# Identity transposes in TensorE's waits of batch 0's attention, and at_l's products behind the others, in a packed attention with a softplus FFN

## The chip, the cores and the metric

The kernel runs on one core of a Trainium2 chip. The metric is the device time of one execution in microseconds (us). Three runs of the kernel before took 799.06, 800.18 and 801.27 us; their median is 800.18 us. All inputs lie in HBM and the output goes back there.

## The reference

q, k and v have the shape 8 x 8 x 576 x 64 (batch, heads, sequence, head size), p has 8 x 8 x 32 x 64. Per batch and head a softmax attention packs k and v into 32 rows for p's queries, and a second attention reads these packed rows with q. The result of all heads goes through an FFN with a softplus in between.

```
p_packed = sm_attn(p, k, v)                # 32 rows for each head
out = sm_attn(q, p_packed, p_packed)       # 576 rows for each head
x = out.transpose(0, 2, 1, 3).reshape(B * S, H * D)    # 4608 x 512
h = x @ w_in                               # w_in 512 x 2048
g = np.maximum(h, 0.0) + np.log1p(np.exp(-np.abs(h)))
return (g @ w_out).astype(np.float32)      # w_out 2048 x 512
```

`sm_attn` scales the scores by 1/8, subtracts the row's maximum, and divides by the sum plus 1e-9. w_in and w_out come in 64-bit floats.

## The kernel before, in words

**Staging.** Batch 0's attention runs first and alone; then the FFN runs batch by batch, in units: a unit is one of the 16 blocks of 128 FFN columns of one batch. RUNS gives their order: blocks 0 to 7 of batch 0, all blocks of batch 1, blocks 8 to 15 of batch 0, then the batches 2 to 7. Between the products of a unit the kernel steps through the attention of the next batch (`attention`, a generator) and, in the first units, through the conversion of the weights (`convert`, a generator too).

**attention(b)** works on two groups of four heads (g = 0, 1). `transposed` makes T_k and T_q: three TensorE transposes into a PSUM bank and a copy on ScalarE. `scores1` multiplies T_k with pT; ScalarE copies the scores (tile a1, printed as a), VectorE takes the maximum, ScalarE the exponential. `a1_transposed` turns the weights on TensorE into the bank psa, and ScalarE copies them to a1T. `packed` multiplies them with v (bank psp). For the second attention `scores2` multiplies T_q with the packed rows (pt), VectorE transposes the scores (L324), `softmax2_exp` and `softmax2_div` normalise them with VectorE and ScalarE, and a last VectorE transpose makes aT (L348). c = 0, 1 are the two halves of the 576 rows.

**convert** makes 32-bit weights out of the 64-bit ones, for each x_i (of w_in) and x_o (of w_out): a DMA load, m and r on ScalarE (L182, L186), t on VectorE (L188, L193), a sum on GpSimd (L201), and for x_o the two parts wo_h (ScalarE, L222) and wo_l (VectorE, L228).

**weights(b)** splits aT into two parts of reduced precision: at_h is a cast on ScalarE (L469), at_l the difference on VectorE (L470), for c = 0 with g = 0, 1, then for c = 1. **make_m** multiplies the packed rows with w_in (bank psm) and splits the product into mh (ScalarE) and ml (VectorE), for two blocks at once in the first units. **gemm1(b, f, res)** then adds, for each half c and in one PSUM accumulation, six products over g: mh with at_h, mh with at_l, ml with at_h. `softplus` reads the result, and two units later `gemm2_tile` multiplies gh and gl with wo_h and wo_l into the bank acc.

**Order.** TensorE's instructions stand as the program writes them. The other engines' queues are ordered by a scheduler when the program is built; each engine then works through its queue in that order. DMA loads are issued on the sync queue. During batch 0's attention `bank` hands out six PSUM banks in turn (four of ps_acc, two of ps_m), afterwards the two of ps_m.

Of the kernel before, what the change touches and what calls it, by code (L numbers as in the profile page):

```python
# [9 lines left out]
F32 = mybir.dt.float32  # L10
# [16 lines left out]
def pack_attention_then_softplus_ffn(  # L27
# [10 lines left out]
    nc = tc.nc  # L38
# [3 lines left out]
    P = 128  # L42
# [3 lines left out]
    C = S // 2  # L46
    G = H * J // P
# [24 lines left out]
    ident = const.tile([P, P], F32, name="ident")  # L72
# [17 lines left out]
    def bank(nm):  # L90
        if spare:
            spare.append(spare.pop(0))
            pool, tag = spare[-1]
            return pool.tile([P, 512], F32, tag=tag, name=nm)
        return ps_m.tile([P, 512], F32, tag="m", name=nm)
# [11 lines left out]
    def pack_transposed(bg, t):  # L107
        for o in range(0, H, HG):
            ps = bank(f"ppt_{bg}_{o}")
            for i in range(HG):  # L110
                nc.tensor.transpose(ps[:D, i * P:(i + 1) * P], t[:, o + i, :], ident)
            dst = pT[:, o:o + HG, :].rearrange("x h j -> x (h j)")
            nc.vector.tensor_copy(dst[:D], ps[:D])
            nc.scalar.copy(dst[D:], ps[:D])
# [41 lines left out]
    def convert(order):  # L156
# [56 lines left out]
        for n in range(len(order) + 1):  # L213
# [13 lines left out]
            if w == "o":  # L227
# [3 lines left out]
                made.add((w, i))  # L231
                yield


    def transposed(nm, b, g, hh):

        src = loaded[nm, b, g]
        ps = bank(f"psT_{nm}_{b}_{g}_{hh}")
        for i in range(HS):
            nc.tensor.transpose(  # L240
                ps[:, i * NP:(i + 1) * NP],
                src[:, hh, 2 * i:2 * i + 2, :].rearrange("x s d -> x (s d)"),
                ident[:NP, :NP],
            )
        dst = work.tile([P, C], F32, tag="T", name=f"T_{nm}_{b}_{g}_{hh}", bufs=4)
        nc.scalar.copy(dst, ps[:, :C])  # L246
        return dst
# [105 lines left out]
    def attention(b):  # L353
# [34 lines left out]
        pp[0] = packed(b, 0, a1T, rs0)  # L388
        load("k", b + 1, 0)
        yield  # L390
        qT.append(transposed("q", b, 0, 0))
        yield
        a1T = work.tile([NP, SI, P], F32, tag="a1T", name=f"a1T_{b}_1", bufs=1)
# [66 lines left out]
    def weights(b):  # L460

        at_h = work.tile([P, G, S], F32R, tag="at_h", name=f"at_h_{b}", bufs=1)
        at_l = work.tile([P, G, S], F32R, tag="at_l", name=f"at_l_{b}", bufs=1)
        res[b]["at"] = (at_h, at_l)
        for c in range(2):
            cols = slice(c * C, (c + 1) * C)
            for g in range(G):
                aT = res[b]["aT"][g, c]
                nc.scalar.copy(at_h[:, g, cols], aT)  # L469
                nc.vector.tensor_tensor(  # L470
                    at_l[:, g, cols], aT, at_h[:, g, cols].bitcast(F32), op=ALU.subtract
                )
# [39 lines left out]
    def gemm1(b, f, res):  # L512

        at_h, at_l = res["at"]
        phs = []
        for c in range(2):
            ph = ps_h.tile([P, 512], F32, tag="h", name=f"ph_{b}_{f}_{c}")
            phs.append(ph[:, :C])
            i = 0
            for g in range(G):  # L520
                mh, ml, o = res["m"][f][g]
                ms = slice(o, o + P)
                cs = slice(c * C, (c + 1) * C)
                for x, y in ((mh, at_h), (mh, at_l), (ml, at_h)):
                    nc.tensor.matmul(  # L525
                        ph[:, :C], x[:, ms], y[:, g, cs],
                        start=(i == 0), stop=(i == 3 * G - 1),
                    )
                    i += 1
        return phs  # L530

    def halves(nm):
# [111 lines left out]
    res = [{"pt": [], "aT": {}, "m": {}} for _ in range(B)]  # L644

    spare += [(ps_acc, "acc")] * NT + [(ps_m, "m")] * 2
    pack_transposed(0, pt)
    due = 0.0
    for st, _ in enumerate(attention(0)):
# [3 lines left out]
            due -= 1  # L653
    make_m(0, 0, m_cols(0), res[0])
    weights(0)

    spare.clear()
    cdue = 0.0
    gs, acc = {}, None
# [94 lines left out]
```

## Time and profile before

| | |
|---|---|
| median of three runs | 800.18 us (799.06 to 801.27) |
| the profiled execution, its own time | 801.79 us |
| its span, first to last instruction | 800.0 us |
| TensorE busy | 761.3 us, 95% |
| VectorE busy | 514.6 us, 64% |
| ScalarE busy | 468.4 us, 59% |
| GpSimd busy | 92.6 us, 12% |
| mean granted TensorE clock over the span | 0.985 |

Busy times are sums over the whole span. The kernel has stages with different limits, so the table alone does not tell what limits a stage; the rows further down are cut by time. The granted clock is a share of 2.4 GHz. Ends of matmuls are modelled, so a row's length on TensorE is that of its last instruction plus the starts before it.

### The profile page before, as it was taken

To read this page: it belongs to the slowest core of one execution; us is meant where nothing else is said; L and a number is where in the kernel's file an instruction comes from. 1 tells how busy PE (TensorE), PEld (TensorE's weight loads), DVE (VectorE), ACT (ScalarE), POOL (GpSimd) and SP (SyncE) were. 2 spreads that over 40 slices of the span, in tenths; PEclk is the share of its full clock that TensorE was granted. 3 is DMA by queue.
4 is the path that set the end of the run, shared out by engine and by line. 5 is a ranking of instruction groups with operands and counts; after the bars stand their busy time and mean duration, and the time that the engine had idled before them with its cause. 6 is when DMAs were issued, how large, how long until landed. Compare 5 with 4: busy or idle time off the path is not lost.

```text
span 800.0 us, 14909 instructions
## 1 busy us (share of the span) xinstructions
PE 761.3 (95%) x5664; PEld 602.2 (75%) x5664; DVE 514.6 (64%) x1180; ACT 468.4 (59%) x1189; POOL 92.6 (12%) x166
## 2 busy tenths in 40 slices
PE   6369998999999999999999999999999999999997
PEld 4246676777788787877788777878778777878886
DVE  2685898855687547764677456764587546764544
ACT  5668787866563565575555465566556355555540
POOL 1412234400000000000000000000000000000010
PEclk9967999999999999999999999999999999999999
DMA  9985655501513112122212122132211210010002
GB/s 230 236 218 161 167 164 162 141 9 55 169 32 83 43 30 61 30 83 60 61 30 64 33 60 60 31 84 60 60 30 28 70 31 1 1 53 1 1 2 66
DMA packets 40519, 59.28 MB, mean 74 GB/s; under 512 B 5120, under 2 KB 32768, under 8 KB 40448
## 3 DMA queue, kind: packets, MB, share of 16 engines
q1 hardware_dynamic: 39904, 58.21, 28.3%
q8 instruction: 44, 0.72, 0.4%
q14 instruction: 27, 0.22, 0.1%
q10 hardware_dynamic: 544, 0.13, 0.1%
HBM read 47.25 MB, written 11.08 MB: 73 GB/s over the span
## 4 chain that ended last, share of the span: by engine, by line
PE 83%; DVE 7%; ACT 4%; DMA 3%; issue 1%; POOL 1%; SPq 0%; ACTq 0%; DVEq 0%; POOLq 0%
PE acc L567 40%; PE ph L525 25%; PE acc_m L567 5%; PE psm L490 4%; PE ps L253 3%; PE psT_k L240 2%; DMA x_o<-in_moe_w_out 2%; PE psT_q L240 2%; PE psp L296 1%; DVE t L193 1%; DVE t L188 1%; DMA x_i<-in_moe_w_in 1%; PE psa L286 1%; ACT m L182 1%; DVE e L553 1%
## 5 line engine op out<-in xcount | busy, mean ns | idle before, releaser
L553 DVE SCALAR_TENSOR_TENSOR e<-ph,e 128x288 f32<-128x288 f32 x256 | 114.4, 454 | 165.0 <-ACT e L551 164.8
L567 PE MATMUL acc<-wo_h,gh 128*128 128x512 f32 x512 | 213.8, 418 | 0.7 <-DVE o L578 0.7
L567 PE MATMUL acc<-wo_l,gh 128*128 128x512 f32 x512 | 201.4, 393 | 0.0
L567 PE MATMUL acc<-wo_h,gl 128*128 128x512 f32 x512 | 201.2, 393 | 0.0
L549 ACT ACTIVATE e<-ph 128x288 f32<-128x288 f32 x256 | 103.0, 403 | 156.2 <-PE ph L525 111.2
L525 PE MATMUL ph<-at_h,mh 128*128 128x288 f32 x512 | 160.2, 313 | 5.3 <-DVE e L553 3.0
L525 PE MATMUL ph<-at_l,mh 128*128 128x288 f32 x512 | 153.0, 299 | 4.6 <-DVE at_l L470 4.6
L525 PE MATMUL ph<-at_h,ml 128*128 128x288 f32 x512 | 152.9, 299 | 0.0
L525 PEld LDWEIGHTS ph<-at_h,mh 128*128 128x128 f32 x512 | 97.6, 191 | 40.2 <-DVE gl L540 12.8
L559 POOL COPY rest<-e 128x64 f32<-128x64 f32 x128 | 47.8, 374 | 594.5 <-DVE e L553 590.5
L567 PEld LDWEIGHTS acc<-wo_h,gh 128*128 128x128 f32 x512 | 96.3, 188 | 23.3 <-issue 9.8
L567 PEld LDWEIGHTS acc<-wo_h,gl 128*128 128x128 f32 x512 | 96.3, 188 | 21.6
L550 ACT ACTIVATE e<-e 128x288 f32<-128x288 f32 (+1 forms) x240 | 109.1, 455 | 3.6
L551 ACT ACTIVATE e<-e 128x288 f32<-128x288 f32 (+1 forms) x240 | 109.5, 456 | 2.1
L567 PEld LDWEIGHTS acc<-wo_l,gh 128*128 128x128 f32 x512 | 96.8, 189 | 10.2
L525 PEld LDWEIGHTS ph<-at_l,mh 128*128 128x128 f32 x512 | 97.9, 191 | 7.2 <-DVE at_l L470 5.0
L525 PEld LDWEIGHTS ph<-at_h,ml 128*128 128x128 f32 x512 | 97.8, 191 | 0.0
L540 DVE TENSOR_TENSOR gl<-e,gh 128x512 fp32r<-128x512 f32 x128 | 88.6, 692 | 6.1
L504 ACT CAST mh<-psm 128x512 fp32r<-128x512 f32 (+1 forms) x76 | 36.2, 521 | 43.0 <-PE psm L490 42.7
L539 DVE CAST gh<-e 128x512 fp32r<-128x512 f32 x128 | 55.8, 436 | 7.0 <-PE acc L567 0.5
L505 DVE TENSOR_TENSOR ml<-psm,mh 128x512 fp32r<-128x512 f32 (+1 forms) x76 | 43.3, 596 | 22.8 <-ACT mh L504 22.7
L246 ACT COPY T_k<-psT_k 128x288 f32<-128x288 f32 x64 | 24.9, 397 | 25.5 <-PE psT_k L240 24.8
(78 smaller groups left out, 818.1 us busy)
## 6 DMA issues: line engine op xcount, KB each, us to landing
k<-in_k SPq DMA_DIRECT2D x16, 576.0 KB, 4.8
v<-in_v SPq DMA_DIRECT2D x16, 576.0 KB, 4.8
q<-in_q SPq DMA_DIRECT2D x16, 576.0 KB, 4.7
x_i<-in_moe_w_in SPq DMA_DIRECT2D x32, 256.0 KB, 4.1
x_o<-in_moe_w_out SPq DMA_DIRECT2D x16, 512.0 KB, 4.0
out<-o SPq DMA_DIRECT2D x21, 192.0 KB, 2.4
out<-o SPq DMA_DIRECT2D x14, 128.0 KB, 2.3
out<-o SPq DMA_DIRECT2D x21, 64.0 KB, 2.0
```

Source lines behind the costliest of these rows:

```text
L240: nc.tensor.transpose(ps[:, i * NP:(i + 1) * NP], src[:, hh, 2 * i:2 * i + 2, :].rearrange("x s d -> x (s d)"), ident[:NP, :NP],)
L504: nc.scalar.copy(mh[:, cols], ps[:, :n])
L505: nc.vector.tensor_tensor(ml[:, cols], ps[:, :n], mh[:, cols].bitcast(F32), op=ALU.subtract)
L525: nc.tensor.matmul(ph[:, :C], x[:, ms], y[:, g, cs], start=(i == 0), stop=(i == 3 * G - 1),)
L539: nc.vector.tensor_copy(hi, x)
L540: nc.vector.tensor_tensor(lo, x, hi.bitcast(F32), op=ALU.subtract)
L549: nc.scalar.activation(es[c], hv[c], AF.Abs)
L550: nc.scalar.activation(e[:, x], e[:, x], AF.Exp, scale=-1.0)
L551: nc.scalar.activation(e[:, x], e[:, x], AF.Ln, bias=1.0)
L553: nc.vector.scalar_tensor_tensor(es[c], hv[c], 0.0, es[c], op0=ALU.max, op1=ALU.add)
L559: nc.gpsimd.tensor_copy(rest[:, rest_at(b, f), r:r + REST], e[:, NT * P:])
L567: nc.tensor.matmul(acc, x[:, cs], y[:, f, :], start=(first and i == 0), stop=(last and i == 2),)
```

## The change

Four groups of transposes are added, written by a new function `busy(n, nm, home)`: n times the 128 x 128 identity is transposed into a PSUM bank that no one reads. Sixteen stand first of all on TensorE (busy_p), fifty behind batch 0's first products with v and ahead of the first transposes of q (busy_q), fifteen ahead of the first unit's gemm1 (busy_at), and twenty-five inside it (busy_at_l, in a bank of ps_acc). In gemm1 of every unit the order of the products is new: mh with at_h and ml with at_h for both g, then mh with at_l. In the first unit both halves c go through the products with at_h, then come the twenty-five transposes, then both halves' products with at_l.

```diff
+    def busy(n, nm, home=None):
+        if home:
+            ps = home[0].tile([P, 512], F32, tag=home[1], name=f"busy_{nm}")
+        else:
+            ps = bank(f"busy_{nm}")
+        for _ in range(n):
+            nc.tensor.transpose(ps[:, :P], ident, ident)
...
         load("k", b + 1, 0)
         yield
+        if b == 0:
+            busy(50, "q")
         qT.append(transposed("q", b, 0, 0))
...
-                for x, y in ((mh, at_h), (mh, at_l), (ml, at_h)):
...
+        early, late = [(1, at_h), (0, at_h)], [(1, at_l)]
+        if (b, f) == (0, 0):
+            for c in range(2):
+                products(c, early, True, False)
+            busy(25, "at_l", (ps_acc, "acc"))
+            for c in range(2):
+                products(c, late, False, True)
+        else:
+            for c in range(2):
+                products(c, early + late, True, True)
...
     spare += [(ps_acc, "acc")] * NT + [(ps_m, "m")] * 2
+    busy(16, "p")
     pack_transposed(0, pt)
...
     weights(0)
+    busy(15, "at")
```

The scheduler also orders the other engines' queues anew. On ScalarE, at the start of attention(0), the copies out of the first transposes stand in this row before (the numbers at the ends of names tell buffers apart):

```order
L114 COPY pT<-ppt_0_125 64x512
L246 COPY T_k_0_0_145<-psT_k_0_0_141 128x288
L114 COPY pT<-ppt_4_132 64x512
L246 COPY T_k_0_1_160<-psT_k_0_1_156 128x288
L246 COPY T_k_0_2_166<-psT_k_0_2_162 128x288
L246 COPY T_k_0_3_183<-psT_k_0_3_179 128x288
L262 COPY a_0_0_139<-ps_0_0_0_187 128x288
```

and after the change in this one:

```order
L256 COPY T_k_0_0_162<-psT_k_0_0_158 128x288
L114 COPY pT<-ppt_0_142 64x512
L114 COPY pT<-ppt_4_149 64x512
L182 ACTIVATE m_164<-x_i_111 128x512
L186 ACTIVATE r_166<-x_i_111 128x512
L256 COPY T_k_0_1_177<-psT_k_0_1_173 128x288
L256 COPY T_k_0_2_183<-psT_k_0_2_179 128x288
L256 COPY T_k_0_3_200<-psT_k_0_3_196 128x288
```

The two steps of the conversion of the first x_i (m and r) now stand ahead of T_k_0_1 to T_k_0_3, and those of the second between the two a copies.

Still on ScalarE, in attention(0), the two copies a1T out of the transposed weights of g = 0, for which the products with v wait, stand so before:

```order
L287 COPY a1T_0_274<-psa_0_0_275 96x384
L287 COPY a1T_0_274<-psa_0_1_292 96x384
L273 ACTIVATE a_0_1_140,z_0_1_290<-a_0_1_140,nm_0_1_272 128x576
L182 ACTIVATE m_211<-x_o_119 128x512
L186 ACTIVATE r_213<-x_o_119 128x512
```

and so after:

```order
L297 COPY a1T_0_291<-psa_0_0_292 96x384
L182 ACTIVATE m_228<-x_o_119 128x512
L186 ACTIVATE r_230<-x_o_119 128x512
L283 ACTIVATE a_0_1_157,z_0_1_307<-a_0_1_157,nm_0_1_289 128x576
L182 ACTIVATE m_255<-x_o_121 128x512
L186 ACTIVATE r_257<-x_o_121 128x512
L222 CAST wo_h<-t_232 128x512
L297 COPY a1T_0_291<-psa_0_1_309 96x384
```

The second a1T copy now stands behind the conversion of two x_o chunks, the exponential of g = 1, and the cast of wo_h.

On TensorE, the m products of batch 0 (psm) and the start of the first unit's gemm1, with the three products of c = 0, g = 0 (bank ph_0_0), stand so before; the three of g = 1 follow, then the six of c = 1 (bank ph_0_1):

```order
L490 MATMUL psm_0_0_546<-w_in_sb,pT 32x256 x4
L490 MATMUL psm_0_1_547<-w_in_sb,pT 32x256 x4
L525 MATMUL ph_0_0_572<-at_h_562,mh_0_0_556 128x288
L525 MATMUL ph_0_0_572<-at_l_563,mh_0_0_556 128x288
L525 MATMUL ph_0_0_572<-at_h_562,ml_0_0_557 128x288
```

and this is the whole of that gemm1 after:

```order
L502 MATMUL psm_0_1_615<-w_in_sb,pT 32x256 x4
L242 MATMUL busy_at<-ident 128x128 x15
L535 MATMUL ph_0_0_656<-at_h_630,mh_0_0_624 128x288 x2
L535 MATMUL ph_0_0_656<-at_h_630,ml_0_0_625 128x288 x2
L535 MATMUL ph_0_1_657<-at_h_630,mh_0_0_624 128x288 x2
L535 MATMUL ph_0_1_657<-at_h_630,ml_0_0_625 128x288 x2
L242 MATMUL busy_at_l<-ident 128x128 x25
L535 MATMUL ph_0_0_656<-at_l_631,mh_0_0_624 128x288 x2
L535 MATMUL ph_0_1_657<-at_l_631,mh_0_0_624 128x288 x2
```

The fifteen transposes stand behind the m products, the eight products with at_h of both halves follow, and the twenty-five transposes stand between these and the four with at_l.

On VectorE, in the stretch from the first scores of q to the last at_l, one step of the conversion (L188 and L193) that stood ahead of the first transpose out of these scores now stands behind it, and the last transpose to aT stands one at_l earlier. On all queues, steps of the conversion change places with neighbours up to the end of batch 1's units.

## Rows read from the trace of the kernel before

**Rows 1.** That is the span cut into stretches of time (us from its start), with the busy time of each engine in a stretch and the count of its instructions, then the granted TensorE clock as a share of full speed, the mean busy share of the DMA engines and GB/s.

```profile
45.00:49.00 4.00, 0.00 (x0) 0.00 (x0) 4.00 (x15) 1.97 (x5) 0.00 (x0) 0.51 0.97 208
...
53.00:69.00 16.00, 14.89 (x90) 10.56 (x96) 8.90 (x21) 11.52 (x28) 3.63 (x5) 0.50 0.57 160
69.00:70.00 1.00, 1.00 (x18) 0.49 (x11) 0.00 (x0) 0.53 (x3) 1.00 (x1) 1.00 0.00 0
...
90.00:140.00 50.00, 45.77 (x319) 35.53 (x320) 47.35 (x108) 38.16 (x82) 17.69 (x18) 1.00 0.57 161
140.00:800.00 660.00, 654.41 (x4778) 523.85 (x4776) 410.98 (x941) 370.75 (x977) 50.61 (x121) 1.00 0.19 49
```

**Rows 2.** That is instructions of one line on TensorE, with nanoseconds of one (minimum/median/maximum), their first and last start in us, and their shape. The k transposes of 0 to 60 us; the transposes of a1 up to 34 us; the same after 70 us; the products with v from 33 to 36 us.

```profile
L240 PE MATMUL psT_k<-ident,k x36: 362/367/423, 7.2 to 55.0; 96*128 96x96 f32 x36
...
L286 PE MATMUL psa<-ident,a x12: 417/421/447, 16.4 to 32.9; 128*96 128x128 f32 x12
...
L286 PE MATMUL psa<-ident,a x12: 271/272/273, 70.3 to 79.2; 128*96 128x128 f32 x12
...
L296 PE MATMUL psp<-v,a1T x48: 219/314/317, 33.9 to 35.0; 96*32 96x64 f32 x48
```

**Rows 3.** That is TensorE's timeline of the first 71 us: start, time up to the end of the last one of a row, operation, count, and in brackets the idle time before and what ended it.

```profile
4.86 1.89 PE L111 MATMUL ppt<-ident,p 128*64 128x128 f32 x8 [4.86 <-DMA p<-in_p]
...
18.68 1.51 PE L296 MATMUL psp<-v,a1T 96*32 96x64 f32 x48 [0.80 <-ACT a1T L287]
31.30 0.71 PE L240 MATMUL psT_q<-ident,q 96*128 96x96 f32 x3 [11.12 <-DMA q<-in_q]
31.80 1.49 PE L286 MATMUL psa<-ident,a 128*96 128x128 f32 x6
...
44.33 0.40 PE L525 MATMUL ph<-at_h,mh 128*128 128x288 f32 x1 [2.16 <-ACT at_h L469]
49.28 0.61 PE L525 MATMUL ph<-at_l,mh 128*128 128x288 f32 x1 [4.55 <-DVE at_l L470]
...
52.56 2.79 PE L240 MATMUL psT_k<-ident,k 96*128 96x96 f32 x12
...
70.32 0.49 PE L286 MATMUL psa<-ident,a 128*96 128x128 f32 x3
```

**Rows 4.** That is the chain of work that ended last, in order of time, from 52.76 to 69.64 us and at 91.47 us: start, us, engine, tile, line. The pieces on TensorE alone.

```profile
52.76 0.49 PE psT_k L240 x3
...
55.56 1.34 PE psm L490 x16
56.91 3.18 PE ph L525 x12
60.09 1.16 PE ps L253 x16
...
63.46 1.22 PE psT_k L240 x6
64.68 2.93 PE ph L525 x12
67.62 1.28 PE acc L567 x3
68.90 0.74 PE ps L253 x16
...
91.47 1.80 PE ph L525 x12
```

**Rows 5.** That is ScalarE's timeline of 9 to 24 us, with the columns of rows 3.

```profile
9.01 1.00 ACT L246 COPY T_k<-psT_k 128x288 f32<-128x288 f32 x3
11.27 0.70 ACT L262 COPY a<-ps 128x288 f32<-128x288 f32 x2 [1.25 <-PE ps L253]
...
19.53 0.78 ACT L273 ACTIVATE a<-a,nm 128x576 f32<-128x576 f32 x1 [0.53 <-DVE nm L268]
...
20.31 0.64 ACT L182 ACTIVATE m<-x_o 128x512 f32<-128x512 f32 x1
20.85 0.66 ACT L186 ACTIVATE r<-x_o 128x512 int32<-128x512 uint32 x1
...
23.68 0.62 ACT L222 CAST wo_h<-t 128x512 fp32r<-128x512 f32 x1 [1.05 <-POOL t L201]
```

**Rows 6.** That is the two DMA issues of the first x_i on the sync queue (nanoseconds of one, first and last start), and the time from an issue to its landing, minimum/median/maximum, us.

```profile
L137 SPq DMA_DIRECT2D x_i<-in_moe_w_in x2: 629/686/742, 2.7 to 3.5; - x2
...
DMA to landing us min/median/max: 8.1/8.3/8.5
```

**Rows 7.** That is ScalarE's and VectorE's timelines of 36 to 52 us, with the columns of rows 3.

```profile
36.41 0.68 ACT L246 COPY T_q<-psT_q 128x288 f32<-128x288 f32 x2
...
48.85 0.43 ACT L469 CAST at_h<-aT 128x288 fp32r<-128x288 f32 x1 [1.14 <-DVE aT L348]
50.93 0.43 ACT L469 CAST at_h<-aT 128x288 fp32r<-128x288 f32 x1 [1.65 <-DVE aT L348]
...
36.69 0.69 DVE L193 SCALAR_TENSOR_TENSOR t<-m,t 128x512 int32<-128x512 int32 x1
37.85 0.85 DVE L324 STREAM_TRANSPOSE a<-ps 128x288 f32<-128x288 f32 x2 [0.47 <-PE ps L253]
...
51.40 0.46 DVE L470 TENSOR_TENSOR at_l<-aT,at_h 128x288 fp32r<-128x288 f32 x1
```

More of the change, by code (lines that the diff above doesn't have):

```diff
@@ L514, in gemm1, with products @@
         at_h, at_l = res["at"]
[L515 to L523, printed above, removed]
-                for x, y in ((mh, at_h), (mh, at_l), (ml, at_h)):
+        phs = [
+            ps_h.tile([P, 512], F32, tag="h", name=f"ph_{b}_{f}_{c}")[:, :C] for c in range(2)
+        ]
+        def products(c, ways, first, last):
+            for w, (hi, y) in enumerate(ways):
+                for g in range(G):
+                    mh, ml, o = res["m"][f][g]
                     nc.tensor.matmul(
-                        ph[:, :C], x[:, ms], y[:, g, cs],
-                        start=(i == 0), stop=(i == 3 * G - 1),
-                    )
-                    i += 1
+                        phs[c], (mh if hi else ml)[:, o:o + P], y[:, g, c * C:(c + 1) * C],
+                        start=first and w + g == 0,
+                        stop=last and w == len(ways) - 1 and g == G - 1,
+                    )
+        early, late = [(1, at_h), (0, at_h)], [(1, at_l)]
[8 more added lines that the diff above has]
+                products(c, early + late, True, True)
         return phs
```

## The prediction

> **What bounds the kernel now.** I read four views in this order: the busy time by stage, the durations of one operation at different times, TensorE's timeline of the first 71 us, and the chain of waits. By stage [rows 1], TensorE is busy for 654.41 of the last 660.00 us, so from 140 us on it is the bound, and whatever happens earlier shifts this part as a whole. From 90 to 140 us VectorE is the bound (47.35 of 50.00 us). Everything that the change adds lies before 58 us, apart from the order of gemm1's products.
>
> TensorE's clock is the point. The granted clock is 0.51 to 0.50 from 45 to 69 us and 1.00 from 69 us on [rows 1], so 1.2 GHz and then 2.4 GHz. The column also reads 1.00 before 45 us, and there the durations speak against it: the k transposes take the same 362 to 423 ns at 7.2 us as at 55 us, where the granted clock is 0.50, and the a transposes take 421 ns up to 33 us but 272 ns after 70 us [rows 2]. The v products fall from 317 to 219 ns between 33.9 and 35.0 us [rows 2]. So TensorE runs at 1.2 GHz until about 34.8 us, at 2.4 GHz until 45, at 1.2 GHz until 69, and at 2.4 GHz after that. The rise at 34.8 came 3.5 us after work set in at 31.30, with transposes alone up to 33.3 [rows 3]; the rise at 69 came 5.5 us after work set in at 63.46 [rows 4]; the fall at 45 came after one matmul in the 3 us since the m products [rows 1, 3].
>
> TensorE's waits in batch 0's attention [rows 3]: 4.86 us for p, 11.12 us for q (q lands at 31.2), 2.16 us for at_h, 4.55 us up to 49.28. On the chain from 52.76 to 69.64 TensorE has eight pieces: 0.49, 1.34, 3.18, 1.16, 1.22, 2.93, 1.28 and 0.74 us [rows 4], together 12.3 us, nearly all at 1.2 GHz. That is what a higher clock could give back.
>
> **The change part by part.** *busy(16, "p").* One transpose at 1.2 GHz costs 0.214 us: six take 1.49, less 0.42 for the last one's length, by 5 [rows 2, 3]. Sixteen are 3.4 us and fit into the 4.86 us wait; they need only the identity. Cost 0.
>
> *The order on ScalarE.* The change also moves the weight conversion in ScalarE's queue, as the order shows. The three copies T_k_0_1 to T_k_0_3 ran at 9.01 us [rows 5]; now m and r of the first x_i stand before them, and x_i has landed only at 3.5 + 8.5 = 12.0 us [rows 6]. m and r take 0.56 each (20.31 to 20.85) [rows 5], so these copies start at 13.1, 4.1 us later. From there I walk the queue with the gaps of [rows 5]: three copies to 14.0, the scores 1.25 later at 15.3, an a copy 0.3, m and r of the second x_i 1.1, an a copy 0.3, four T_k copies 1.2, so 18.25; scores of g=1 at 19.5, the a transposes and the first a1T copy at 20.7. The second a1T copy now stands behind m, r, exp (0.8), m, r and the cast of wo_h. m starts at 20.7 and that cast comes 3.4 us after its m (20.31 to 23.68) [rows 5], so at 24.1, the a1T copy at 24.6 to 25.0, and the last v products end at 25.7 instead of 20.2 [rows 3]. Before, 11 us of waiting for q would have covered this whole.
>
> *busy(50, "q").* It stands between these v products and q's transposes, so it starts at 25.7 with q due at 31.2. At 1.2 GHz all fifty take 10.7 us and end at 36.4; at 2.4 GHz, 0.11 us each (three in 0.49 less 0.27, by 2 [rows 2, 3]), 5.4 us and 31.1. Before 25.7 TensorE has been nearly idle for 4 us, so it starts low; with the lags seen, 3.5 to 5.5 us, the rise leaves 34 to 24 transposes at 0.108: end at 32.8 to 33.8. I take 33.3, 2.0 us after q's transposes start now. What follows is then at 2.4 GHz, and the path goes through ScalarE: T_q, two a1T, T_q, m, r, two T_q, 3.1 us of copies and a start of 0.5, then 0.8 to the first transpose out of the scores (36.41 to 37.85, less the two copies [rows 7]). That transpose starts at 37.7, against 37.85 now. The delay and the clock cancel; ends -0.6 (rise early) and, all low, +3.5.
>
> *From there to at_h.* VectorE works almost without pause from 37.85 to 51.86 [rows 7] (4.00 of 4.00 us from 45 to 49 [rows 1]), so its queue counts. By the order a step of the conversion that ran ahead of this stretch (L188 and L193, the latter 0.69 at 36.69 [rows 7]) now stands inside it, while a small sum and a maximum leave the part up to the first aT: I take +0.5 us, between 0 and 1.1. The last aT goes ahead of one at_l: -0.4 us. The last at_h, ready at 50.93 + 0.43 = 51.36 now [rows 7], is ready at about 51.3.
>
> *busy(15, "at").* 1.6 us at 2.4 GHz, in the 2.16 us before at_h at 44.33 [rows 3]; were it 3.2 us at 1.2 GHz, the end at 45.4 would still lie ahead of at_h of g=1, for which the next product waits (below). Cost 0.
>
> *at_l last and busy(25, "at_l").* By the order the 25 transposes stand behind all eight early products, and the last three of these need the last at_h [rows 7], ready only 0.5 us before the last at_l (51.40 + 0.46). So the wait of 4.55 us stays empty; it is now for at_h of g=1, ready at 48.85 + 0.43 = 49.28 [rows 7]. TensorE idles for nearly 5 us from 44.4 on, more than before the fall at 45, so the clock falls. The transposes start at 51.3 + 0.7 = 52.0, at 1.2 GHz, after every input is there or nearly so: 25 cost 4.4 us (rise 3.5 us into them) to 5.3 us (no rise before their end). The four at_l products take 0.5 to 1.0. gemm1 of the first unit ends at 56.9 to 58.2, I take 57.6, against 52.56 now [rows 3]: **+5.0 us**. Bounds: +2.3 if the clock is still high (25 x 0.108 = 2.7), +6.2 with the late end of each step.
>
> *The clock after that.* The transposes and products make 6 us of closed work from 52, longer than both lags, so the clock is high by about 56 to 58 instead of 69. The pieces on the chain then shrink: 12 products take 1.80 at 2.4 GHz (91.47 us) for 3.18 and 2.93, and the rest about half except the last: 0.24 + 0.67 + 1.38 + 0.42 + 0.6 + 1.13 + 0.6 = 5.0 us. But ScalarE is busy for 11.52 of the 16.00 us from 53 to 69 [rows 1], so no more than 4.5 us can go before it is late next, at its e and T_k steps. I take **-4.5 us**; bounds -3.0 (one rise that comes 2 us late, or gaps in ScalarE's queue) and -6.2 (half of the 12.3, if part of ScalarE's conversion is done during the 25 transposes).
>
> *The order of the products elsewhere.* gemm1 keeps the number of its products and of its weight loads in every unit; only their order changes, and after 140 us TensorE has 5.6 us of pauses in all [rows 1] that it could touch. Cost 0. Moves of conversion steps between 55 and 140 us come from the same order; each is 0.4 to 1.3 us, in both directions: 0, with an end of +3.5.
>
> The Trainium skill, page "TensorE: Matmul & The Clock Gate", section "Part 4: PE-mode transpose", speaks against the whole change: it says that transposes do not bring in the high clock, since they don't count as busy work in the way that products do. The trace disagrees as far as it goes: of the 3.5 us before the rise at 34.8, the first 2.0 hold nothing but transposes [rows 3]. By the rule the sum would be that of the second rival.
>
> **Sum.** +5.0 - 4.5 = +0.5 us. The profiled execution took 801.79 us (span 800.0); it would take 802.3. It lies 0.2% above the median of the three runs, 800.18, which gives **800.7 us**.
>
> **The rivals.** *The clock holds (faster).* If the 15 transposes keep 2.4 GHz through the wait up to 49.28, gemm1 ends 2.3 us later, and with 4.5 to 6.2 back the time is 796.3 to 798.0. For it: before, the clock fell with fewer transposes ahead. Against: the idle stretch is longer than the one it fell in.
>
> *Transposes don't raise the clock (slower).* Then busy_q ends at 36.4 at 1.2 GHz and the scores come 3.5 to 4.2 us late, busy_at_l costs 5.3 and the at_l products 1.0, and the stage to 69 stays as slow as it is: 4 + 0.3 + 5.8 = +10 us, **810 us**. It decides from the point where the clock gives back less than 2.6 us, that is with a rise later than some 62 us. Against: the rise at 34.8.
>
> *ScalarE's order costs again (slower).* One more x_i or x_o that lands after the place of its m in the queue, like the 4.1 us at T_k_0_1, in the stage up to 140, where VectorE has 2.65 us of slack in 50 to make it good [rows 1]: +3 to +5 on top, 803.7 to 805.7. For it: the order has such moves in every unit; against: after 57 us the loads have had 5 us more to land.
>
> **How the numbers follow.** Forecast 0.50 (799 to 802.5, with a tail of 0.05 above), the clock holds 0.20, the order costs 0.18, no rise 0.12. A measurement of this kernel tells 0.3%, 2.4 us, from no change. Faster by more: 0.20, the first rival; slower by more: 0.12 + 0.18 + 0.05 = 0.35; within: 0.45. The range leaves out the rise that fails and little more: 796.5 to 806.0.
>
> **What would show it.** Right: the copies T_k_0_1 at about 13 us, busy_q from about 25.7 to 33.3 with its durations falling from 421 to 272 ns, busy_at_l starting after the last at_h at about 52 and not in the wait before 49, gemm1 ending near 57.6, and the granted clock at 1.00 ten us earlier than 69. Wrong: busy_q over before q lands, busy_at_l before 49 us, a clock of 1.00 all through, or one that is still 0.50 after 60 us.

## The result, and the profile after

The changed kernel took 806.00 us in the median of four runs, beside 800.72 us for the kernel before on the same chip: ratio 1.0067 [1.0045, 1.0089]. Timed again on another chip it took 806.94 us beside 800.88: 1.0076 [1.0057, 1.0096]. So it is slower by 5 to 6 us, and more than 0.3%. One of the four ran at a granted clock of 0.555 in the mean and took 1244.91 us (the others 805.55 to 806.43, median 805.58; the ratio leaves it out); the rows below are from another execution of the changed kernel, which took 807.71 us with a span of 805.9.

The span of the changed kernel by stretches (columns as in [rows 1]; the engines stand in the order TensorE, its weight loads, VectorE, ScalarE, GpSimd):

```profile
26.00:30.60 4.60, 4.60 (x28) 4.55 (x23) 3.42 (x7) 2.91 (x5) 2.02 (x2) 0.50 1.04 305
30.80:34.00 3.20, 3.20 (x32) 3.20 (x31) 0.61 (x1) 0.00 (x0) 1.34 (x2) 1.00 1.12 193
45.00:49.00 4.00, 0.40 (x1) 0.19 (x1) 4.00 (x15) 1.83 (x6) 0.00 (x0) 0.85 0.70 168
53.90:58.00 4.10, 4.10 (x21) 4.10 (x20) 2.60 (x3) 0.30 (x1) 2.29 (x2) 0.50 0.45 149
58.10:68.20 10.10, 7.24 (x77) 5.17 (x75) 5.02 (x12) 9.05 (x23) 1.92 (x3) 1.00 0.48 110
68.30:71.60 3.30, 3.30 (x16) 3.30 (x17) 2.55 (x8) 2.09 (x6) 1.34 (x1) 0.50 0.68 162
...
90.00:140.00 50.00, 44.17 (x309) 33.09 (x308) 47.36 (x107) 36.93 (x78) 15.68 (x17) 1.00 0.63 173
140.00:800.00 660.00, 657.65 (x4816) 527.13 (x4815) 415.39 (x947) 374.86 (x986) 52.50 (x123) 1.00 0.19 49
```

From 140 us on nothing is new: TensorE is the bound, and the loss up to there shifts the rest as a whole. Before that the clock does rise early, at 30.7 inside the fifty transposes and at 58.0 inside the twenty-five, but it falls again from 68.3 to 71.7 us. In a second profile (17) it rises at 54.9 already, and is low again from 61.7 to 65.1, from 68.5 to 71.9 and from 78.7 to 82.2. The kernel before has part of the early clock itself in one of its two profiles: in (18) it reads 1.00 from 52.9 to 56.3 and from 59.7 to 63.1.

TensorE's timeline of the changed kernel (columns as in [rows 3]):

```profile
1.36 3.67 PE L242 MATMUL busy_p<-ident 128*128 128x128 f32 x16 [1.36 <-POOL ident masks.py:199]
4.83 1.91 PE L111 MATMUL ppt<-ident,p 128*64 128x128 f32 x8
7.26 1.21 PE L250 MATMUL psT_k<-ident,k 96*128 96x96 f32 x12 [0.52 <-DMA k<-in_k]
...
15.35 2.18 PE L250 MATMUL psT_k<-ident,k 96*128 96x96 f32 x12
...
25.25 0.87 PE L306 MATMUL psp<-v,a1T 96*32 96x64 f32 x24 [3.33 <-ACT a1T L297]
26.05 7.94 PE L242 MATMUL busy_q<-ident 128*128 128x128 f32 x50
33.83 0.41 PE L250 MATMUL psT_q<-ident,q 96*128 96x96 f32 x3
...
42.97 1.85 PE L242 MATMUL busy_at<-ident 128*128 128x128 f32 x15
45.93 0.40 PE L535 MATMUL ph<-at_h,mh 128*128 128x288 f32 x1 [1.10 <-ACT at_h L481]
51.47 0.61 PE L535 MATMUL ph<-at_h,mh 128*128 128x288 f32 x1 [5.14 <-ACT at_h L481]
...
53.88 4.92 PE L242 MATMUL busy_at_l<-ident 128*128 128x128 f32 x25
58.56 0.78 PE L535 MATMUL ph<-at_l,mh 128*128 128x288 f32 x4
59.19 0.66 PE L250 MATMUL psT_k<-ident,k 96*128 96x96 f32 x6
60.18 0.47 PE L250 MATMUL psT_k<-ident,k 96*128 96x96 f32 x3 [0.33 <-ACT T_k L256]
61.04 0.47 PE L250 MATMUL psT_k<-ident,k 96*128 96x96 f32 x3 [0.40 <-ACT T_k L256]
62.00 0.84 PE L502 MATMUL psm<-w_in_sb,pT 64*32 64x256 f32 x16 [0.49 <-ACT T_k L256]
```

Beside [rows 3]: busy_p fits, q's transposes start at 33.83 instead of 31.30, the wait inside gemm1 is 5.14 instead of 4.55 us and stays empty, and the twenty-five stand behind it. Then TensorE waits for ScalarE at each step.

ScalarE's copies that the prediction placed, in the changed kernel (columns as in [rows 3]):

```profile
13.20 0.97 ACT L256 COPY T_k<-psT_k 128x288 f32<-128x288 f32 x3
...
24.73 0.47 ACT L297 COPY a1T<-psa 96x384 f32<-96x384 f32 x1
```

Since the first us differ from profile to profile (q's transposes, where they wait for q's data, start anywhere from 29.7 to 32.7 us), the table counts from the end of the last at_h: us from there to the first product into acc, from that to the first ph product of unit 4 (units counted from 0), and on to units 5, 9, 13, 24 and the end of the span. The names in the first column are those of the experiments below.

| kernel | last at_h | acc | unit 4 | 5 | 9 | 13 | 24 | end | span |
|---|---|---|---|---|---|---|---|---|---|
| before | 51.4 | 16.0 | 13.6 | 10.4 | 22.7 | 23.3 | 60.2 | 602.4 | 800.0 |
| before, again (18) | 51.5 | 14.6 | 13.1 | 10.4 | 22.7 | 23.3 | 60.2 | 602.5 | 798.2 |
| changed (1) | 52.9 | 18.6 | 14.8 | 9.1 | 25.1 | 22.8 | 60.2 | 602.5 | 805.9 |
| changed, again (17) | 52.8 | 17.6 | 15.9 | 9.1 | 24.8 | 22.8 | 60.2 | 602.4 | 805.6 |
| order only (5) | 52.6 | 16.4 | 12.7 | 13.4 | 24.7 | 22.8 | 60.2 | 602.4 | 805.2 |
| first unit (9) | 50.6 | 16.1 | 12.7 | 14.5 | 24.2 | 23.7 | 61.7 | 602.4 | 805.8 |
| other units (10) | 51.9 | 15.3 | 13.3 | 10.4 | 22.7 | 23.5 | 60.1 | 602.4 | 799.7 |
| queues kept (13) | 53.0 | 11.4 | 14.5 | 10.3 | 22.7 | 23.3 | 60.1 | 602.4 | 797.8 |
| queues moved (14) | 50.2 | 13.6 | 13.8 | 9.8 | 23.3 | 24.9 | 60.5 | 602.9 | 799.0 |
| kept, k and q (16) | 50.4 | 12.8 | 13.0 | 10.4 | 22.7 | 23.3 | 60.2 | 602.5 | 795.2 |

The two profiles of each kernel average to: +1.4 us up to the last at_h, +2.8 to the first acc, +2.0 to unit 4, -1.3 to unit 5, +2.25 to unit 9, -0.5 to unit 13, nothing after it; together 6.65, the difference of the mean spans (805.75 and 799.1).

### The profile page after: what moved, and what is told of

Its sections match the earlier page's. It is cut to its first block, busy times and chain, and to the rows that moved or that the text cites. A ratio compares the mean times of both kernels' runs of the same rounds, so it can differ in the third digit from the quotient of the medians.

```text
span 1243.1 us, 15114 instructions
## 1 busy us (share of the span) xinstructions
PE 1223.1 (98%) x5770; PEld 811.4 (65%) x5770; DVE 523.3 (42%) x1180; ACT 487.9 (39%) x1189; POOL 91.0 (7%) x166
## 4 chain that ended last, share of the span: by engine, by line
PE 96%; ACT 1%; DVE 1%; DMA 1%; SPq 0%; issue 0%; POOL 0%; ACTq 0%
PE acc L589 48%; PE ph L535 27%; PE acc_m L589 6%; PE psm L502 4%; PE ps L263 3%; PE psT_q L250 2%; PE psT_k L250 2%; PE psa L296 1%; PE psp L306 1%; PE busy_q L242 1%; DMA x_i<-in_moe_w_in 1%; PE busy_at_l L242 0%; PE psx L319 0%; ACT m L182 0%; DVE a L343 0%; ACT T_k L256 0%
## 5 line engine op out<-in xcount | busy, mean ns | idle before, releaser
L589 PE MATMUL acc<-wo_h,gh 128*128 128x512 f32 x512 | 310.2, 606 | 0.0
L589 PE MATMUL acc<-wo_h,gl 128*128 128x512 f32 x512 | 295.8, 578 | 0.0
L589 PE MATMUL acc<-wo_l,gh 128*128 128x512 f32 x512 | 294.5, 575 | 0.0
L589 PEld LDWEIGHTS acc<-wo_h,gl 128*128 128x128 f32 x512 | 116.3, 227 | 76.1 <-issue 34.8
L535 PEld LDWEIGHTS ph<-at_h,mh 128*128 128x128 f32 x512 | 113.1, 242 | 74.6 <-issue 52.7
L589 PEld LDWEIGHTS acc<-wo_h,gh 128*128 128x128 f32 x512 | 113.9, 222 | 63.0 <-issue 41.6
L589 PEld LDWEIGHTS acc<-wo_l,gh 128*128 128x128 f32 x512 | 117.7, 230 | 43.4 <-issue 28.2
L535 PEld LDWEIGHTS ph<-at_l,mh 128*128 128x128 f32 x512 | 117.8, 252 | 3.5
L535 PEld LDWEIGHTS ph<-at_h,ml 128*128 128x128 f32 x512 | 117.1, 251 | 3.5
L256 ACT COPY T_q<-psT_q 128x288 f32<-128x288 f32 x64 | 25.3, 399 | 84.1 <-PE psT_q L250 83.9
```

The lines of the kernel that those rows point to most:

```text
L535: nc.tensor.matmul(phs[c], (mh if hi else ml)[:, o:o + P], y[:, g, c * C:(c + 1) * C], start=first and w + g == 0, stop=last and w == len( ...
L589: nc.tensor.matmul(acc, x[:, cs], y[:, f, :], start=(first and i == 0), stop=(last and i == 2),)
```

## The experiments

Four theories stood at the start. **A**: the twenty-five stand behind the wait and cost 5 us that the clock doesn't give back. **B**: what is moved early (T_k behind the first x_i, busy_q past q's landing) is the loss. **C**: the new order of products costs, by itself or by what the scheduler makes of it in the other queues. **D**: the fifty do harm to the clock. Later C was cut in two, C1 (the queues) and C2 (the order of products itself).

**1. The changed kernel, profiled.**

> The changed kernel once more, for a profile with the clock at 2.4 GHz in the FFN. Theory A (the 25 transposes come after the wait and cost 5 us, the clock gives less back than 4.5 us): gemm1 of the first unit ends at 56 to 58 us, and the stage to the first acc products ends 4 to 6 us later than before. Theory B (the new queue order costs: x_i's conversion ahead of T_k, busy_q past the landing of q): busy_q ends after 34 us, the last at_h is ready 2 us or more later than 51.4. Theory C (the new order of gemm1's products costs in every unit): the loss is spread over the span, some 0.04 us in each of 128 units.

807.71 us in one run. The rows are those above: the table finds the loss at three places, and none of the four theories has all three.

**2 to 6. Groups of transposes left out.** All are edits of the changed kernel; 5 leaves only the new order of products and what the scheduler makes of it.

```diff
-    busy(16, "p")                            # 2, 5, 6
...
-            busy(50, "q")                    # 4, 5, 6
...
-            busy(25, "at_l", (ps_acc, "acc"))   # 3, 5
...
-    busy(15, "at")                           # 5
```

> Without the sixteen transposes at the start; by the order ScalarE's and VectorE's queues then stand as before up to the first unit. Theory B: the v products end near 20 us, busy_q ends before q lands, and the time is 802 to 804. Theory A: it stays within 1.5 us of the changed kernel, 804.5 to 806.5. Theory C: 805 to 806.

> Without the twenty-five transposes in gemm1; at_l's products stay last. Theory A: gemm1 ends 4 to 5 us earlier, and if the clock still rises late the time is 801 to 802.5. Theory B: within 1.5 us of the changed kernel. Theory C: 805 to 806.

> Without the fifty transposes ahead of q; ScalarE's early queue stays that of the changed kernel. Theory B: q's transposes start when q lands, at about 31, and the time is 803 to 804. Theory A: no gain, 805 to 807, since the clock then rises 1 us later in q's stage. Theory C: 805 to 806.

> No transposes at all; only the new order of gemm1's products, with the queue order that the scheduler then makes (the same as before up to the first unit on ScalarE and VectorE, 190 to 200 places different after that). Theory A (the transposes behind the wait, and a clock that falls again at 68 us because TensorE waits for ScalarE): 799 to 801.5, no difference from the kernel before. Theory C (the product order or the queue order behind the first unit costs): 802.5 or more.

> Only the fifteen and the twenty-five transposes; the queue order is the same as in the run without the sixteen. Theory A: q's stage runs as before, at_h ready at 51.4 to 51.9, gemm1 ends at 57.3 to 58.0, the clock rises within the twenty-five; 803.5 to 805. Theory D (it is the fifty that keep the clock low in q's stage, 13.7 us at 1.2 GHz in the run without the sixteen, and that costs most): 801 to 802.5.

| left out | median, us | ratio to before |
|---|---|---|
| 2: busy_p | 806.16 | 1.0073 [1.0051, 1.0094] |
| 3: busy_at_l | 803.92 | 1.0046 [1.0029, 1.0064] |
| 4: busy_q | 806.50 | 1.0080 [1.0048, 1.0111] |
| 5: all four | 805.50 | 1.0067 [1.0045, 1.0088] |
| 6: busy_p, busy_q | 805.92 | 1.0087 [1.0056, 1.0118] |

A is right only by half: without the twenty-five (3) it is about 2 us faster, which is less than A's range asked for and fits none of the theories, and run 6 lies above both of its ranges. B falls: without busy_p the copies T_k and the v products are back where they were (v ends at 20.7 us), and the time is the same; so it is without busy_q. D falls with run 4. The surprise is 5: with no transpose added at all the kernel is as slow as the changed one. TensorE's longest waits from 67 to 140 us in that kernel, where the columns are what waited, for what, us in total, times, longest (e is a step of the softplus on VectorE):

```profile
PE ph L533 <- DVE e L572: 4.2, 5, 1.5
PE psT_q L250 <- ACT T_q L256: 3.6, 1, 3.6
```

Before, the largest in this stretch is 3.0 us in four waits for e, and the one wait for T_q is 0.4 us. Behind the 3.6 us the clock falls too, so the work behind the wait is slower as well (columns as in [rows 1]; two stretches of the order-only kernel):

```profile
85.00:89.40 4.40, 1.15 (x8) 0.79 (x6) 2.60 (x7) 3.08 (x7) 1.60 (x2) 1.00 0.78 174
89.40:92.80 3.40, 3.02 (x22) 1.48 (x22) 2.06 (x6) 1.99 (x5) 1.37 (x2) 0.50 0.71 187
```

**7 and 8. Transposes inside the real waits.** The wait in gemm1 is for at_h of g = 1, behind one product of g = 0. Run 7 puts the transposes there and drops busy_p, busy_q and busy_at_l; 8 adds 8, 4 and 4 in batch 1's k stage.

```diff
-            for c in range(2):
-                products(c, early, True, False)
-            busy(25, "at_l", (ps_acc, "acc"))
+            for c, n in ((0, 40), (1, 14)):
+                products(c, [(1, at_h)], True, False, gs=(0,))
+                busy(n, f"gap_{c}", (ps_acc, "acc"))
+                products(c, [(1, at_h)], False, False, gs=(1,))
+                products(c, [(0, at_h)], False, False)
```

> Neither the sixteen nor the fifty; the transposes are put into the wait itself: fifteen ahead of gemm1, forty between the first and the second product with at_h of c=0, fourteen between those of c=1, none behind. Theory A: gemm1 ends at 52.3 to 53 as before, the clock stays high from about 35 to past 60, the first acc product starts at 64 to 66 instead of 67.4 and the time is 797 to 799.5. If the gain of the clock in this stage is nothing (ScalarE bound through), 800 to 801.5. If the order behind costs 2 us, that much more.

> The same, with sixteen more transposes in the waits for ScalarE of batch 1's k stage (8, 4 and 4), where the clock fell at 68 us in the changed kernel. Theory A: no fall between 53 and 75 us, first acc product 1 us or more earlier than without them if gemm1 of the third unit ran at 1.2 GHz there; 796.5 to 799. If TensorE is not what is late there, the same as the run before.

7: 799.31 us, 0.9997 [0.9977, 1.0016]; 8: 802.66 us, 1.0034 [1.0015, 1.0052]. 7 lies at the upper end of A's range, 8 above both of its ranges. From the last at_h, 7 takes 14.2 us to the first acc and 8 takes 12.7, where the two profiles of the kernel before take 16.0 and 14.6. In 8 unit 4 comes 25.7 us after the last at_h, against 29.6 and 27.7, but unit 9 after 62.1, against 62.7 and 60.8: what the clock won, 2 to 4 us, is gone again within five units but for 0.7 us at most.

**9 to 12. The order of products, cut in two.** None of 9, 10 and 12 has an added transpose. 9 has the new order in batch 0's first unit alone, 10 in all units but this one; 11 is run 7 with the old order in the other units; 12 is run 5 with two q copies on VectorE.

```diff
+        if (nm, b, g) == ("q", 1, 0) and hh in (2, 3):      # 12
+            nc.vector.tensor_copy(dst, ps[:, :C])
+        else:
+            nc.scalar.copy(dst, ps[:, :C])
```

> No added transposes; the new order of products (all products with at_h of both halves, then those with at_l) in batch 0's first unit alone, every other unit as before. Up to the step from unit 4 to unit 5 its ScalarE queue is that of the order-only kernel: the q copy of batch 1 (T_q, hh 2) stands behind a conversion step's m and r of an x_i. Theory C1 (the queues: what the scheduler makes of the changed first unit puts a T_q copy behind an x_i that lands at 88): as slow as the order-only kernel, 804 to 806 us, first acc near 69.0, unit 5 near 95, with TensorE waiting over 3 us for a T_q at 86 to 90. Theory C2 (the order of products in every unit costs by itself, small waits in each): 800 to 802, no such wait, unit 5 near 92.

> No added transposes; batch 0's first unit as before, the new order of products in the 127 others. Its ScalarE queue equals that of the kernel before for the first 156 entries, past the copies T_q of batch 1. C1: 799 to 802 us, within 0.3% of before, first acc at 67.4, unit 5 near 91.4, no wait of over 2 us for a T_q. C2: 803 to 806, lost a little at a time over the units up to 140 us and beyond.

> The run with transposes in the real waits for at_h (15 ahead, 40 and 14 inside), with the products of every unit but the first back in the order of before. C1: the same queue up to the T_q copies as in the order-only kernel, so the 3 us won by the first acc (64.5) are partly lost by unit 9; 797 to 800 us. C2: 794 to 796.5, since no other unit has the new order and the gain of 3 to 4 us by the first acc stays whole.

> The order-only kernel with two of batch 1's four q copies of g=0 (hh 2 and 3) made on VectorE instead of ScalarE, so that they no longer stand behind the conversion of an x_i on ScalarE. C1: the wait of 3.6 us at 86 to 90 is gone or under 1.5 us, unit 5 near 92.5 instead of 95.1, 801 to 803.5 us. C2 or another cause: the time stays at 804.5 to 806.5, with the loss somewhere else by unit 9.

9: 805.88 us, 1.0066 [1.0042, 1.0090]. 10: 799.39, 0.9984 [0.9966, 1.0003]. 11: 802.22, 1.0028 [1.0008, 1.0047]. 12: 803.15, 1.0043 [1.0020, 1.0067]. The order of products is free in 127 units (10), and the whole loss hangs on the one unit in which it moves the other queues (9). It isn't lost in that unit: by the table run 9 is as fast as before up to unit 4, and loses 4.1 us from there to unit 5 and 3.4 more up to unit 24. So it is C1, and C2 falls. Run 11 missed C1's range too, by 2.2 us above.

Run 12's time lies in C1's range, but not for the reason given: from unit 4 to 5 it takes 13.3 us, as long as run 5 (from 5 to 9 it is 22.4 instead of 24.7). The wait for T_q is gone, and one as long stands in its place. TensorE's row in 12 (pp is the packed rows of a group, which VectorE scales out of the bank psp):

```profile
88.29 0.44 PE L250 MATMUL psT_q<-ident,q 96*128 96x96 f32 x3 [3.60 <-DVE pp L317]
```

VectorE's queue there, in the kernel before, then in run 9 (which has the same order there as 12, but T_q on ScalarE); columns as in [rows 3]:

```profile
84.97 0.68 DVE L228 TENSOR_TENSOR wo_l<-t,wo_h 128x512 fp32r<-128x512 f32 x1
85.57 0.47 DVE L304 TENSOR_SCALAR pp<-psp,rs 128x64 f32<-128x64 f32 x2
86.03 0.82 DVE L553 SCALAR_TENSOR_TENSOR e<-ph,e 128x288 f32<-128x288 f32 x2
87.47 0.69 DVE L228 TENSOR_TENSOR wo_l<-t,wo_h 128x512 fp32r<-128x512 f32 x1 [0.62 <-ACT wo_h L222]
```

```profile
82.98 0.68 DVE L228 TENSOR_TENSOR wo_l<-t,wo_h 128x512 fp32r<-128x512 f32 x1
85.47 0.69 DVE L228 TENSOR_TENSOR wo_l<-t,wo_h 128x512 fp32r<-128x512 f32 x1 [1.80 <-ACT wo_h L222]
86.08 0.81 DVE L573 SCALAR_TENSOR_TENSOR e<-ph,e 128x288 f32<-128x288 f32 x2
86.81 0.46 DVE L314 TENSOR_SCALAR pp<-psp,rs 128x64 f32<-128x64 f32 x2
```

And ScalarE's and GpSimd's in run 9:

```profile
84.81 0.62 ACT L222 CAST wo_h<-t 128x512 fp32r<-128x512 f32 x1 [1.29 <-POOL t L201]
85.34 0.68 ACT L571 ACTIVATE e<-e 128x576 f32<-128x576 f32 x1
85.92 0.65 ACT L182 ACTIVATE m<-x_i 128x512 f32<-128x512 f32 x1
86.47 0.65 ACT L186 ACTIVATE r<-x_i 128x512 int32<-128x512 uint32 x1
87.02 0.38 ACT L256 COPY T_q<-psT_q 128x288 f32<-128x288 f32 x1
```

```profile
83.23 1.55 POOL L201 TENSOR_TENSOR t<-t,r 128x512 int32<-128x512 int32 x1 [2.74 <-DVE t L193]
```

Before, pp stood ahead of the second wo_l; now it stands behind it, and this wo_l waits for wo_h, which waits for GpSimd's sum. T_q stands behind the same wo_h on ScalarE. Both end at 87.3 and 87.4 us, so to take one of them away (run 12) leaves the other. In the order-only kernel both engines' queues have the same order there, with the second wo_l at 87.79 after a wait of 1.80 for wo_h, pp at 89.13 and T_q at 89.35.

**13 to 16. The queues kept.** These have the old order of products everywhere. 13 and 14 differ in one number; 15 and 16 add to 13. The edit against the kernel before, with the lists of products written out:

```diff
+    busy(15, "at")
...
+            for c, n in ((0, 40), (1, 7)):           # 14: (1, 14)
+                products(c, [(1, at_h)], True, False, gs=(0,))
+                busy(n, f"gap_{c}", (ps_acc, "acc"))
+                products(c, [(1, at_l), (0, at_h)], False, False, gs=(0,))
+                products(c, [(1, at_h), (1, at_l), (0, at_h)], False, True, gs=(1,))
...
+        if b == 1:                                    # 15, 16: at three places
+            busy(4, "k0", (ps_acc, "acc"))
...
+        if b == 0:                                    # 16
+            busy(50, "q")
```

> Every product in the order of before, all units. Added are identity transposes in TensorE's real waits in batch 0's first unit: 15 ahead of its products, 40 after the first product with at_h of g=0 of the first half, 7 at the same place of the second half. VectorE's queue is entry for entry that of before, ScalarE's but for one neighbouring pair (the first e and the cast beside it). C1 (moved queues cost the five us): the gain by the first acc (64.5 instead of 67.4) stays to the end, 796 to 798 us, unit 24 at 194.5 to 195. Rival: the gain is lost by unit 9 whatever the queues, since ScalarE and VectorE bound that stretch, 799 to 802.

> The run before it with 14 transposes instead of 7 at the last place; all else on TensorE the same. With those seven the scheduler's queues move: on VectorE the pp of batch 1 (g=1) stands behind the e of unit 4 and the wo_l ahead of it, on ScalarE T_q behind an x_i. C1: 800 to 803 us, 3 to 5 us over its neighbour, with a wait for pp or T_q of over 1 us at unit 4 that the neighbour hasn't. Rival: within 1 us of its neighbour, since seven transposes are 1.5 us at the lower clock inside a wait.

> The run with the queues kept, and 4, 4 and 4 transposes more in batch 1's k stage (before and after its g=1 k copies), where TensorE waits for ScalarE and the granted clock fell again at 55 and 62; the queues stay as before. If the clock then holds to 84 as in the run with 8, 4 and 4: 795.5 to 797 us, up to 1 less than the run without them. Rival: they stand ahead of T_k's transposes on TensorE and cost what they give, 796.5 to 798.5.

> The run before it with the change's fifty transposes ahead of q's; the queues stay as before. If the fifty fit into the wait for the softmax and the clock's early rise is lost again in the next waits: within 0.7 us of the run before it. Rival (they push q's transposes back by 2 us as in the changed kernel and every later step with them): 1.5 to 2.5 us more.

13: 798.83 us, 0.9978 [0.9967, 0.9989]. 14: 802.44, 1.0031 [1.0016, 1.0047]. 15: 798.11, 0.9974 [0.9954, 0.9994]. 16: 797.47, 0.9974 [0.9960, 0.9988]. 13 lies 0.8 us above C1's range, 14 inside it and 3.6 above 13, as C1 has it; 15 gained 0.7 and falls to its rival, although the clock held from 58.1 to 126.3 us in its profile; 16 is within 0.7 of 15. Seven transposes cost 3.6 us in the median, of which they are themselves at most 0.76 (14 took 1.69 us in run 14, 7 took 0.93 in run 13). The rest is laid to the queues, which are all else that differs in the program: VectorE's queue as built, at unit 4, in 13 and then in 14:

```
L228 TENSOR_TENSOR wo_l<-t_1117,wo_h 128x512
L314 TENSOR_SCALAR pp_1_1071<-psp_1_1046,rs_1_888 128x64 x2
L575 SCALAR_TENSOR_TENSOR e_4_1036<-ph_4_0_1022,e_4_1036 128x288
```

```
L228 TENSOR_TENSOR wo_l<-t_1124,wo_h 128x512
L562 TENSOR_TENSOR gl_3_1009<-e_3_972,gh_3_1008 128x512
L188 TENSOR_SCALAR t_1203<-m_1199 128x512
L193 SCALAR_TENSOR_TENSOR t_1203<-m_1199,t_1203 128x512
L575 SCALAR_TENSOR_TENSOR e_4_1043<-ph_4_0_1029,e_4_1043 128x288
L575 SCALAR_TENSOR_TENSOR e_4_1043<-ph_4_1_1030,e_4_1043 128x288
L314 TENSOR_SCALAR pp_1_1078<-psp_1_1053,rs_1_895 128x64 x2
```

With it, TensorE's wait for pp is 1.46 us in 14 and 0.60 in 13:

```profile
83.56 0.44 PE L250 MATMUL psT_q<-ident,q 96*128 96x96 f32 x3 [1.46 <-DVE pp L314]
```

```profile
84.01 0.45 PE L250 MATMUL psT_q<-ident,q 96*128 96x96 f32 x3 [0.60 <-DVE pp L314]
```

But this wait is not the loss: by the table the stretch from unit 4 to 5 takes 9.8 us in 14 and 10.3 in 13. From unit 5 to the end 14 takes 711.6 us, 13 takes 708.5, and there TensorE waits longer. Its waits for e and o (the output on its way out of acc) from 85 to 205 us in 14, and then that for e in 13 (columns as in the waits above):

```profile
PE ph L536 <- DVE e L575: 5.5, 5, 1.5
PE acc L589 <- DVE o L615: 1.0, 1, 1.0
```

```profile
PE ph L536 <- DVE e L575: 3.0, 4, 1.8
```

Which moved operation makes these waits was not tried. From the last at_h to unit 5 the two profiles differ by 1.0 us, and there at_h itself comes at 53.0 in 13 and 50.2 in 14.

16 is the fastest kernel of the study, 2.7 us under before, timed on the same chip, and some 8 under the changed kernel, with the fifty of the change in it: where the queues stand still they do no harm. That it is faster than before by more than 0.3% is not shown.

**17 and 18. Both kernels again.**

> The changed kernel as it is. If the 1.5 us before the last at_h are the start's spread: the last at_h anywhere from 50 to 53, and the stages behind it as in the first profile, 18.6 us from there to the first acc, 14.8 to unit 4, 9.1 to unit 5, 25.1 to unit 9, 22.8 to unit 13. If they are the change's (the first x_i's m ahead of T_k on ScalarE): the last at_h at 52.5 to 53.3 again. 804.5 to 806.5 us either way.

> The kernel before as it is, for a second profile. If the start spreads by itself: the last at_h anywhere from 49.8 to 53.2; from there 16.0 us to the first acc, 13.6 to unit 4, 10.4 to unit 5, 22.7 to unit 9, each within 0.5. If the change alone moved it: within 0.5 of 51.4.

806.94 us, 0.4 above its range, and one run of 800.04. The last at_h came at 52.8 and 51.5 us, as in the first profiles of the two. These 1.4 us lie inside a spread, though: in the kernels in which q's transposes wait for q's data, they start at 29.7 to 32.7 us, and the last at_h comes 20.1 to 20.8 us later, at 49.8 to 53.0. With the changed kernel's early queue and the fifty (1, 3, 17) they start behind the fifty, at 33.7 to 34.0, and the last at_h comes at 52.8 to 53.2. So the 1.4 us hold against the two profiles of before, where q's transposes start at 31.3 and 31.4; against an execution in which q lands early they would be more, against a late one next to nothing. About 0.5 of them arise up to the first transpose out of q's scores (38.31 and 38.17, against 37.85 and 37.58), and 0.9 from there to the last at_h (14.6 us twice, against 13.5 and 13.9). VectorE shows something of the second part, in both profiles of the changed kernel (this is run 17):

```profile
38.95 0.49 DVE L188 TENSOR_SCALAR t<-m 128x512 int32<-128x512 int32 x1
...
40.65 0.67 DVE L193 SCALAR_TENSOR_TENSOR t<-m,t 128x512 int32<-128x512 int32 x1
...
41.61 1.45 DVE L343 TENSOR_TENSOR a<-a,m 128x288 f32<-128x288 f32 x1
```

One step of the conversion more than before (L188 and L193) stands in the stretch between q's first scores and the last at_l, and a VectorE operation that takes 0.44 us elsewhere took 1.45. In the first profile of the changed kernel (1.44 us) it ran beside a sum on GpSimd:

```profile
41.60 1.27 POOL L201 TENSOR_TENSOR t<-t,r 128x512 int32<-128x512 int32 x1 [2.31 <-ACT T_q L256]
```

Run 4, without the fifty, has neither in that stretch, and its last at_h is at 52.0, 20.1 us after q's transposes start, as in the kernel before.

Run 18 took 14.6 us from the last at_h to the first acc, where 16.0 within 0.5 was expected: this stage of the kernel before differs from execution to execution, as its clock does.

## Why the prediction was wrong

By its own steps:

- *busy_p, cost 0.* Right: 1.36 to 5.03 us, in the wait for p; without it the time is the same (run 2).
- *The order on ScalarE at the start.* Right: the copies T_k at 13.20 (13.1 predicted), the second a1T copy at 24.73 (24.6), the v products end at 26.1 (25.7).
- *busy_q.* Right: 26.05 to 33.99 (25.7 to 33.3), with the rise inside it. The first transpose out of q's scores comes 0.5 us later than forecast (38.31 and 38.17, for 37.7). The rule of the Trainium skill that the prediction set against the change (page "TensorE: Matmul & The Clock Gate", section "Part 4: PE-mode transpose") does not hold for these transposes: the granted clock goes from 0.50 to 1.00 while TensorE had done nothing but transposes of the identity for 4.7 us. Some v products stand ahead of these, up to 26.1 us; at the start of the span there is nothing but transposes (busy_p and p's), and the twelve k transposes behind them take 1.21 us, where twelve more at 15.35 us, at a granted clock of 0.50, take 2.18. Whether the page means the same kind of transposes as these, which the profile lists as MATMUL, no run here shows. The rival built on the rule falls.
- *From there to at_h, +0.5 and -0.4.* Too small: +0.9, which with the 0.5 above makes +1.4 against the two profiles of before. The conversion step is inside the stretch as foreseen; that one VectorE operation would lose 1.0 us was not.
- *busy(15, "at"), cost 0.* Right: TensorE still waits 1.10 us for at_h behind it.
- *busy_at_l.* The mechanism was right: behind the wait, starting at the lower clock, gemm1's end 6.4 and 4.9 us after the last at_h instead of 1.4, so +5.0 and +3.5 (+5.0 predicted). The rival "the clock holds" falls: the wait stayed empty.
- *The clock after that, -4.5.* Mis-sized, and the first failed step. From gemm1's end to the first acc it is 12.2 and 12.7 us, against 14.7 and 13.2 before: it gave back 1.4 on average. The prediction saw that ScalarE would be late next, and then counted on it to keep up: TensorE waits 2.85 us for T_k and a between 59 and 68.2 us, ScalarE is busy for 9.05 of 10.10 us, and then the clock falls again. Together with the step above this is +2.8 up to the first acc; run 3, without the twenty-five, needs 16.5 us there instead of 18.1 and is 2 us faster.
- *Moves of conversion steps between 55 and 140 us, 0 with an end of +3.5.* The second failed step: +2.5 in the changed kernel from the first acc to unit 13 (2.0 - 1.3 + 2.25 - 0.5), and 3.9 in the order-only kernel (against the mean of before). The prediction put this term at nothing because single moves of 0.4 to 1.3 us go in both directions; it did not follow what a moved operation waits for and what now stands behind it. This is the third rival in kind ("ScalarE's order costs again", 803.7 to 805.7, 0.18), but not by the mechanism it named: in the order-only kernel pp and T_q wait behind wo_l and wo_h, which wait for a chain through GpSimd, and no x_i that lands late is needed.
- *The order of products elsewhere, 0.* Right (run 10).

By the terms: 5.0 - 4.5 + 0 = 0.5 was predicted, with the steps up to at_h cancelling; 1.4 + 4.2 - 1.4 + 2.5 = 6.7 was measured in the profiles, 5.3 and 6.1 between the medians. Leaving out gives another cut of the same loss: the new order alone costs as much as the whole change (runs 5 and 9), and the four groups of transposes together next to nothing on top.

What stays open: the waits of the changed kernel from unit 5 to 9 (2.3 us for e in three waits and 0.7 for T_q, before 0.9 for e in two) are laid to the queues because each kernel whose queues match before's in this stretch (10, 13, 16) has 22.7 us there, and 5 and 9 have 24.7 and 24.2; 12, the order-only kernel with two copies on VectorE, has 22.4. Which single place in the changed kernel's queues makes them was not tried. That the steps up to at_h cost 1.4 us rests on two profiles of each kernel.

## What to carry to other kernels

Where a scheduler orders the other engines' queues, a change on one engine is two changes: compare the queues as built before pricing it, follow each moved operation to what it waits for and to what now stands behind it, and look for a form of the edit that leaves the queues as they are (here seven transposes fewer, runs 14 and 13, were worth 3.6 us). A clock that rises earlier gives back only what the next late engine lets through, so price it by that engine's gaps, not by the clocked engine's busy time. Put filler into the wait that is there, ahead of the instruction that waits, and read which input that instruction waits for last.

## What the runs showed of the hardware

- Behind 4.7 us of nothing but transposes of a 128 x 128 identity in fp32 the granted clock went from 0.50 to 1.00, at 30.7 us in the changed kernel; behind the transposes at the start of its span, with no product ahead of them, twelve k transposes took 1.21 us instead of 2.18. Sixteen took 3.67 us at the lower clock; at the higher one fourteen took 1.69 us and seven 0.93, so 0.109 each.
- A VectorE operation on 128 x 288 took 1.45 us instead of 0.44 when it ran beside a GpSimd sum, in two profiles of two; others of the same line at 39.92 and 46.41 us (run 17) took 0.44. Two VectorE transposes at 38.31 us in the first profile also ran beside such a sum (38.02 to 39.29) and took 0.85 together, no more than elsewhere, so not every VectorE operation was slowed; the cause was not tested.
